# Sequence transforms of batches 1 to 3 of an FFT and MLP chain: three float32r products of two-part tables and folds in place of one float32 product

## The chip, the cores and the metric

The kernel runs on one core of a Trainium2 chip. The metric is device time in microseconds (us) of one execution. Times come from repeated executions; the profile is one further execution with the hardware profiler on. Engines are named as the profile names them: PE (TensorE, with PEld for its weight loads), DVE (VectorE), ACT (ScalarE), POOL (GpSimd), SP (SyncE, which here issues most DMAs).

## The reference

A two-dimensional Fourier transform of a real input, of which the real part is kept, then two feed-forward blocks:

```python
def _attn_ref(x):                       # x: (4, 3072, 256) float32
    X = np.fft.fft(x, axis=1)
    X = np.fft.fft(X, axis=2)
    return X.real.astype(np.float32)

def _moe_ref(x, w_in, w_out):           # (256, 2048), (2048, 256), drawn as float64
    h = x @ w_in
    g = np.maximum(0.01 * h, h)
    return (g @ w_out).astype(np.float32)

def _moe2_ref(x, mu_k, mu_r, w_k, w_v, w_r):
...
    k = np.maximum(xk @ w_k, 0.0)
    v = k * k @ w_v
    r = 1.0 / (1.0 + np.exp(-(xr @ w_r)))
    return (r * v).astype(np.float32)
```

## The kernel before, in words

**Four batches, four classes.** The transform along the 3072 positions of a batch uses the symmetry of real input. The positions are folded on each other (lines 162 to 221), so that a batch needs four products of a folded input with cosine or sine tables: kinds Pe, Qe, Po and Qo. Each kind is a sum over 768 rows, done as two halves of three 128-row pieces: `fft_a` (line 234) multiplies the first three pieces with the first table of the kind, `fft_b` (line 246) the other three with the second table. The result is 128 x 386. From the two halves ACT and DVE make two results each, which belong to classes A1, A2 (from Pe, Qe) and G1, G2 (from Po, Qo). The transform along the 256 channels is merged into `w_in` when the kernel starts.

**Steps.** A class is worked through in 16 steps, one for each 128 of the 2048 hidden columns, so a batch has 64 steps, numbered by `i` in the main loop. A step (`step`, line 537) puts on PE six products for the current hidden columns (three in `mm_b`, line 495, and three for the next step in `mm_a`, line 483) and twelve products with `w_out` (line 506) for the step two earlier. All of these are float32r: a float32 value is split by `hi_lo` (line 81) into two float32r parts, a leading part rounded by ACT and the rest by a DVE subtraction, and three products of parts stand for one product of float32. In a step DVE does `d` (line 547), `ev` (line 488, which `mm_b` of the next step waits for) and `gl` (line 527), ACT does `gh` and two leaky activations. After the 256 steps comes the second block, lines 816 to 872, which the change does not touch.

**What stands among the steps.** The sequence transforms are float32 products, three in each half, and the profile shows each of them as two PE instructions. Po is done at steps 2 and 3 of batch 0 and at steps 0 and 1 of the others, Qo at steps 10 and 11 or 3 and 4; Pe and Qe of the next batch at steps 53, 54 and 56, 57. `fft_a` is put behind the products of its step on PE, `fft_b` behind those of the step after. Pe has one extra float32 product with `e7p` (line 241), for the positions that fold on themselves.

**Tables.** There are eight tables of 128 x 3 x 386 float32 (579 KB each, `load_tab`, line 150), loaded by SP's queue into four rotating buffers, again for every batch. A buffer is loaded when PE has done its last product with it.

**Folds of the next batch.** For batch b+1 they go on during batch b, in six groups g. SP's queue loads half of the data into `eo` and `xl` (`first`, line 168), POOL's queue adds the other parts by four accumulating DMAs (`second`, line 180, each behind the one before it on the same tile), and DVE ends the group with three operations (`fin`, line 200): step 1 the difference of the `xl` halves into `eo` (line 202), steps 2 and 3 the sum into `plus` and the difference into `minus` (lines 204 and 206). The 18 `fin` steps are spread over the main loop's steps from f0 to f1: from 17 to 52 in batch 0, from 8 to 52 in the others. `first(0)`, `first(1)` and `second(0)` are issued behind `fft_b` of Qo.

**Other work among the steps.** At steps 53 to 57 and 0 to 4 a piece of the second block's weights is turned from float64 into two float32r parts (`w2_steps`, lines 96 to 145: DVE, ACT and two POOL operations). At step 1 of a class ACT copies the results of the class before out of PSUM.

The order on every engine is the order of the program text (the schedule is manual), and each engine takes its instructions in that order.

Of the kernel before, what the change touches and what calls it, by code (L numbers as in the profile page):

```python
# [17 lines left out]
P = 128  # L18
# [37 lines left out]
@with_exitstack  # L56
def fft_mlp_kernel(ctx, tc, xa, xb, x7, x8, x87, tb, alt, ce, so, mu, w_in, w_out, w_k, w_v, w_r, out):
    nc = tc.nc
# [103 lines left out]
    def fold_ops(b):  # L162
        plus = fft.tile([P, 6, 2, P], F32, tag="plus", bufs=1, name=f"plus{b}")
        minus = fft.tile([P, 6, 2, P], F32, tag="minus", bufs=1, name=f"minus{b}")
        folded[b] = {"Pe": plus[:, :, 0], "Qe": minus[:, :, 1], "Po": minus[:, :, 0], "Qo": plus[:, :, 1]}
        st, eo = {}, {}

        def first(g, p=None):
            if b == 0:
                t = st[g] = p.tile([P, 2, 2, D], F32, tag="xl", bufs=2 if p is fft else 4, name=f"xl{b}_{g}")  # L170
                Q.dma_start(t[:, 0], xa[b, g])
                Q.dma_start(t[:, 1], xb[b, g, :, :, 0:D])
            else:
                eo[g] = fft.tile([P, 2, 2, P], F32, tag="eo", bufs=2, name=f"eo{b}_{g}")
# [37 lines left out]
        def fold7(E=V):  # L212
            t = st["x7"]
            e7 = fft.tile([1, 2, P], F32, tag="e7", bufs=1, name=f"e7_{b}")
            o7 = fft.tile([1, 2, P], F32, tag="o7", bufs=1, name=f"o7_{b}")
            E.tensor_tensor(e7, t[:, :, :P], t[:, :, P:], op=ALU.add)
            E.tensor_tensor(o7, t[:, :, :P], t[:, :, P:], op=ALU.subtract)
            E.tensor_tensor(e7p[0:1], e7[:, 0], e7[:, 1], op=ALU.add)
            E.tensor_tensor(plus[0:1, 0, 1], o7[:, 0], o7[:, 1], op=ALU.subtract)

        return first, second, full, fin, load7, fold7

    folded, classes = {}, {}

# [7 lines left out]


    def fft_a(b, kind):
        t0 = KINDS[kind][0]
        src = folded[b][kind]
        ps = ps_s.tile([P, 512], F32, tag="s", name=f"f{b}{kind}")
        for c in range(3):
            T.matmul(ps[:, :JP], src[:, c], tabs[t0][:, c], start=(c == 0), stop=(c == 2 and kind != "Pe"))
        if kind == "Pe":  # L240
            T.matmul(ps[:, :JP], e7p, altt, start=False, stop=True)
        ev = work.tile([P, PJ], F32, tag="fv", bufs=2, name=f"fe{b}{kind}")
        act_copy(ev[:, :JP], ps[:, :JP])
        return ps, ev

    def fft_b(b, kind, ps, ev):
        _, t1, k1, k2 = KINDS[kind]
        src = folded[b][kind]
        for c in range(3):
            T.matmul(ps[:, :JP], src[:, 3 + c], tabs[t1][:, c], start=False, stop=(c == 2), skip_group_check=True)  # L250
# [129 lines left out]
    tabs = {}  # L380
    tcount = [0]

    def next_tabs(n=2):
        for _ in range(n):
            k = TORD[tcount[0] % 8]
            tcount[0] += 1
            tabs[k] = load_tab(k)

# [12 lines left out]
    for n, g in enumerate((0, 2, 1, 5, 3, 4)):  # L401
        first(g, fft if n < 2 else rows)
        if n == 2:
# [4 lines left out]
            Q.dma_start(altt[0:1], alt)  # L408
    next_tabs(2)
    w_out_load(0)  # L410
    next_tabs(2)
    w_in_load(2, True)
# [35 lines left out]
    wout[0][2]()  # L448
    next_tabs(2)
    w_in_parts(3)  # L450
    wout[1][1]()
    fft_b(0, "Qe", *qe)
    next_tabs(2)
    cur = split_class(0, A1, "P") + split_class(0, A1, "Q")
# [261 lines left out]
    for b in range(B):  # L716

        po_u, qo_u, f0, f1 = (2, 10, 17, 52) if b == 0 else (0, 3, 8, 52)
        pe_u, qe_u = 53, 56
        done = 0  # L720
        for ti, c in enumerate(CL):
# [3 lines left out]
            for u in range(NF):  # L725
# [10 lines left out]
                if b == 0 and ti == 0:  # L736
                    boot(u)
                if i == po_u:
                    half = fft_a(b, "Po")
                if i == po_u + 1:  # L740
                    fft_b(b, "Po", *half)
                    if b + 1 < B and b > 0:
                        next_tabs()
                if b == 0 and i == 6:
                    half = c_a(c8m, "c", False)
                if b == 0 and i == 7:
                    c_b(c8m, "d", G1, *half)
                    next_tabs()
                if i == qo_u:
                    half = fft_a(b, "Qo")  # L750
                if i == qo_u + 1:
                    fft_b(b, "Qo", *half)
                    if b + 1 < B:
# [4 lines left out]
                        second(0)  # L758
                        next_tabs()
                    else:  # L760
                        fft.release()
                        w2_alloc()
                if b + 1 < B:
                    while f0 <= i and done < 18 and done * (f1 - f0) < 18 * (i - f0 + 1):
                        g, q = divmod(done, 3)
                        fin(g, q + 1)
                        done += 1
                        if q == 0 and g < 5:
                            second(g + 1)
                        if q == 2 and g < 4:  # L770
                            first(g + 2)
                        if done == 12:
                            fold7(G)
                    if i == pe_u:
                        half = fft_a(b + 1, "Pe")
                    if i == pe_u + 1:
                        fft_b(b + 1, "Pe", *half)
                        next_tabs()
                    if i == qe_u:
                        half = fft_a(b + 1, "Qe")  # L780
                    if i == qe_u + 1:
                        fft_b(b + 1, "Qe", *half)
                        next_tabs()
                if b == 0 and i == 50:
# [155 lines left out]
def dft_tables():  # L940
# [31 lines left out]

    return f(tb), f(alt), f(lay(ce) / 256), f(lay(so) / 256)

# [33 lines left out]
```

## Time and profile before

| | us |
|---|---|
| median of 3 runs (lowest to highest) | 1549.6 (1549.31 to 1549.88) |
| the profiled execution, its own time | 1552.51 |
| span of the profiled execution, first to last instruction | 1550.6 |
| PE busy in the span | 1519.2 (98%) |
| DVE busy | 1064.5 (69%) |
| ACT busy | 917.0 (59%) |
| POOL busy | 161.8 (10%) |

The span is cut in 40 equal slices in the page. PE is busy in nine tenths or more of every slice but the first. The granted clock of PE is a tenth or more under full speed in the first slice alone, and its mean over the span is 0.992. The chain of work that ended last is made of PE for 94% of the span.

The profile's times of single matmuls include their run through the array, so neighbours overlap: what a product costs is read from the distance of starts, not from its duration.

### The profile page before, as it was taken

How to read it: one execution, taken by the hardware profiler on the slowest of the kernel's cores; microseconds unless marked ns; L12 is line 12 of the kernel's file. 1: busy time of each engine (PE TensorE's matmuls, PEld its weight loads, DVE VectorE, ACT ScalarE, POOL GpSimd, SP SyncE). 2: the span in 40 equal slices, each digit the busy share in tenths (PEclk: the TensorE clock that was granted, in tenths of full speed). 3: DMA queues.
4: the chain of work that ended last, by engine and by line, in shares of the span. 5: the costliest groups of instructions: out<-in, count | busy, mean ns of one | idle time of the engine just before them, and what ended most of it. 6: DMA issues, size and time to landing. Idle time of an engine off the chain costs nothing.

```text
span 1550.6 us, 22458 instructions
## 1 busy us (share of the span) xinstructions
PE 1519.2 (98%) x8418; PEld 1473.9 (95%) x8418; DVE 1064.5 (69%) x1783; ACT 917.0 (59%) x1761; POOL 161.8 (10%) x144
## 2 busy tenths in 40 slices
PE   5999999999999999999999999999999999999999
PEld 2789998999998999999999999999999999999998
DVE  7777775566775567766577675777777776777775
ACT  2666655556665555655566666666666666666664
POOL 4333110031200122200010000000000000000000
PEclk8999999999999999999999999999999999999999
DMA  7426412363402363212311001111111111111100
GB/s 245 154 72 135 81 31 77 108 136 57 80 26 90 99 118 57 56 42 74 107 53 26 22 21 42 41 50 49 48 50 42 42 42 41 42 42 42 41 21 31
DMA packets 75320, 102.12 MB, mean 66 GB/s; under 512 B 10798, under 2 KB 55870, under 8 KB 75210
## 3 DMA queue, kind: packets, MB, share of 16 engines
q1 hardware_dynamic: 55562, 88.85, 18.5%
q0 software_dynamic: 19648, 11.83, 5.9%
q8 instruction: 66, 1.08, 0.3%
q14 instruction: 44, 0.36, 0.1%
HBM read 72.83 MB, written 27.83 MB: 65 GB/s over the span
## 4 chain that ended last, share of the span: by engine, by line
PE 94%; DMA 2%; DVE 2%; issue 1%; ACT 1%; SPq 0%; POOL 0%; ACTq 0%; POOLq 0%; DVEq 0%
PE o L506 33%; PE kps L816 17%; PE v L857 17%; PE ps L495 8%; PE ps L483 8%; PE rps L865 4%; DMA xl<-in_xb 2%; PE wps L321 1%; DMA eo<-in_xa 0%; DMA xl<-in_xa 0%; PE cps L363 0%; PE cps L372 0%; DVE ev L488 0%; DVE d L547 0%; PE wps L323 0%
## 5 line engine op out<-in xcount | busy, mean ns | idle before, releaser
L547 DVE SCALAR_TENSOR_TENSOR d<-ev,ps 128x384 f32<-128x384 f32 (+1 forms) x256 | 142.0, 555 | 216.9 <-PE ps L495 216.4
L76 ACT ACTIVATE gh<-g 128x768 fp32r<-128x768 f32 (+1 forms) x256 | 216.3, 845 | 80.9 <-PE o L506 78.6
L820 ACT ACTIVATE rl<-kps 128x384 f32<-128x384 f32 x254 | 125.0, 492 | 218.5 <-PE kps L816 218.3
L79 ACT ACTIVATE g<-ps 128x384 f32<-128x384 f32 (+1 forms) x256 | 126.2, 493 | 211.6 <-DVE d L547 211.5
L527 DVE TENSOR_TENSOR gl<-g,gh 128x768 fp32r<-128x768 f32 (+1 forms) x256 | 249.5, 975 | 1.5 <-ACT gh L76 1.0
L821 DVE SCALAR_TENSOR_TENSOR k<-kps,rl 128x384 f32<-128x384 f32 x254 | 141.6, 558 | 137.7 <-ACT rl L820 133.8
L506 PE MATMUL o<-gh,uoh 128*128 128x384 f32 (+1 forms) x1024 | 230.4, 339 | 0.0
L506 PE MATMUL o<-gl,uoh 128*128 128x384 f32 (+1 forms) x1024 | 229.0, 338 | 0.0
L506 PE MATMUL o<-gh,uol 128*128 128x384 f32 (+1 forms) x1024 | 228.7, 337 | 0.0
L506 PEld LDWEIGHTS o<-gh,uoh 128*128 128x128 f32 x1024 | 184.3, 189 | 0.0
L506 PEld LDWEIGHTS o<-gh,uol 128*128 128x128 f32 x1024 | 183.8, 189 | 0.0
L506 PEld LDWEIGHTS o<-gl,uoh 128*128 128x128 f32 x1024 | 183.2, 188 | 0.0
L488 DVE SCALAR_TENSOR_TENSOR ev<-cb,w,ps 128x384 f32<-128x384 f32 (+1 forms) x256 | 157.2, 614 | 0.8 <-PE ps L483 0.8
L83 DVE TENSOR_TENSOR k2l<-k,k2h 128x384 fp32r<-128x384 f32 x254 | 139.6, 550 | 0.4 <-ACT k2h L76 0.4
L857 PE MATMUL v<-k2l,wvh 128*128 128x384 f32 x510 | 135.1, 336 | 0.0
L857 PE MATMUL v<-k2h,wvh 128*128 128x384 f32 x510 | 135.1, 336 | 0.0
L857 PE MATMUL v<-k2h,wvl 128*128 128x384 f32 x510 | 135.1, 336 | 0.0
L79 ACT ACTIVATE g<-d 128x384 f32<-128x384 f32 (+1 forms) x256 | 132.3, 517 | 0.0
L76 ACT ACTIVATE k2h<-k 128x384 fp32r<-128x384 f32 x254 | 131.3, 517 | 0.0
L816 PE MATMUL kps<-mh,wkh 128*128 128x384 f32 x508 | 129.6, 336 | 1.3 <-ACT mh L76 0.7
L816 PE MATMUL kps<-ml,wkh 128*128 128x384 f32 x508 | 129.5, 336 | 0.0
L816 PE MATMUL kps<-mh,wkl 128*128 128x384 f32 x508 | 129.4, 336 | 0.0
(295 smaller groups left out, 2501.3 us busy)
## 6 DMA issues: line engine op xcount, KB each, us to landing
out_dram<-o SPq DMA_DIRECT2D x31, 384.0 KB
y<-yo SPq DMA_DIRECT2D x24, 384.0 KB
xl<-in_xa SPq DMA_DIRECT2D x24, 256.0 KB
xa<-y SPq DMA_DIRECT2D x16, 384.0 KB
tab_a<-in_tb SPq DMA_DIRECT2D x8, 579.0 KB
tab_b<-in_tb SPq DMA_DIRECT2D x8, 579.0 KB
tab_c<-in_tb SPq DMA_DIRECT2D x8, 579.0 KB
tab_d<-in_tb SPq DMA_DIRECT2D x8, 579.0 KB
```

The costliest lines, as they stand in the source:

```text
L76: A.activation(o, i, ACTF.Copy)
L79: A.activation(o, i, ACTF.Prelu, alpha=0.01)
L83: V.tensor_tensor(lo, src, hi.bitcast(F32), op=ALU.subtract)
L483: T.matmul(x["ps"][:, :n], l[:, f], r[:, :n], start=(i == 0), stop=(i == 2))
L488: V.scalar_tensor_tensor(x["ev"][:, :n], x["cb"][:, :n], w128[:, u:u + 1], x["ps"][:, :n], op0=ALU.mult, op1=ALU.add)
L506: T.matmul(po[s][h][:, :n], w[:, u % HF, h * P:(h + 1) * P], g[:, s, :n], start=(u == 0 and i == 0), stop=(u == NF - 1 and i == 2))
L527: V.tensor_tensor(gl[:, :, :n], x["g"][:, :, :n], x["gh"][:, :, :n].bitcast(F32), op=ALU.subtract)
L547: V.scalar_tensor_tensor(d[:, :n], x["ev"][:, :n], 2.0, x["ps"][:, :n], op0=ALU.mult, op1=ALU.subtract)
L816: T.matmul(ps[:, :J], w[:, k, sl], x[:, k], start=(i == 0), stop=(i == 5))
L820: A.activation(r, ps[:, :J], ACTF.Relu)
L821: V.scalar_tensor_tensor(k2, ps[:, :J], 0.0, r, op0=ALU.max, op1=ALU.mult)
L857: T.matmul(vps[m][:, :J], w[:, f, m * P:(m + 1) * P], x, start=(f == 0 and i == 0), stop=(f == NK - 1 and i == 2))
```

## The change

For batches 1 to 3 each float32 product of a sequence transform becomes three float32r products: leading part of the fold by leading part of the table, leading part of the fold by rest of the table, rest of the fold by leading part of the table (`fft_mm`). Batch 0 keeps float32 products and float32 tables.

- Tables in two parts (`tbs`, 128 x 2 x 3 x 386, 1158 KB each) are computed on the host and loaded one by one by **POOL's** queue (`load_tab`), into **two** buffers. Batch 0's float32 tables come in pairs into the same two buffers (`load_pair_tab`), by SP's queue as before.
- The folds keep `eo` (the sums in place 0, the differences in place 1) for all six groups in one tile `pm`; `fin` steps 2 and 3 are gone for batches 1 to 3. Instead `fft_src` makes the 128 x 384 sum or difference `t` for one half of one kind (DVE), and splits it into `sh` (ACT) and `sl` (DVE). It is issued one step before `fft_a` for the first half and in the step of `fft_a` for the second.
- For batches 1 to 3 Po moves from steps 0, 1 to steps 1, 2 and Qo from 3, 4 to 4, 5. The six remaining `fin` operations (line 202 before, 214 after) of a batch go from step 17 to 50 in batch 0, and from **14** to 50 (from 8 to 52 before) in the others.

```diff
+    def load_pair_tab(k0, k1):
+        t = fft.tile([P, 2, 3, JP], F32R, tag="tab", bufs=2, name=f"tab_{k0}").bitcast(F32)
+        for i, k in enumerate((k0, k1)):
+            Q.dma_start(t[:, i], tb[TAB[k]])
+            tabs[k] = t[:, i]
+
     def load_tab(k):
-        t = fft.tile([P, 3, JP], F32, tag="tab", bufs=4, name=f"tab_{k}")
-        Q.dma_start(t, tb[TAB[k]])
-        return t
+        t = fft.tile([P, 2, 3, JP], F32R, tag="tab", bufs=2, name=f"tab_{k}")
+        G.dma_start(t, tbs[TAB[k]])
+        tabs[k] = t
...
     def fold_ops(b):
-        plus = fft.tile([P, 6, 2, P], F32, tag="plus", bufs=1, name=f"plus{b}")
-        minus = fft.tile([P, 6, 2, P], F32, tag="minus", bufs=1, name=f"minus{b}")
...
+        pm = fft.tile([P, 6, 2, 2, P], F32, tag="pm", bufs=1, name=f"pm{b}")
...
+            for g in range(6):
+                eo[g] = pm[:, g]
+            folded[b] = pm, o7s
...
+    def fft_src(b, kind, h):
+        pm, o7s = folded[b]
+        i = 0 if kind[0] == "P" else 1
+        t = work.tile([P, 3, P], F32, tag="fv", bufs=2, name=f"t{b}{kind}{h}")
+        hi = fft.tile([P, 3, P], F32R, tag="sh", bufs=2, name=f"sh{b}{kind}{h}")
+        lo = fft.tile([P, 3, P], F32R, tag="sl", bufs=2, name=f"sl{b}{kind}{h}")
+        s = pm[:, 3 * h:3 * h + 3, i]
+        V.tensor_tensor(t, s[:, :, 0], s[:, :, 1], op=ALU.add if kind in ("Pe", "Qo") else ALU.subtract)
...
+        hi_lo(hi, lo, t)
+        srcs[b, kind, h] = hi, lo
+
+    def fft_mm(b, kind, h, ps, stop):
...
+            hi, lo = srcs.pop((b, kind, h))
+            terms = [(w[:, c], t[:, i, c]) for c in range(3) for w, i in ((hi, 0), (hi, 1), (lo, 0))]
+        for n, (w, x) in enumerate(terms):
+            T.matmul(ps[:, :JP], w, x, start=(h == 0 and n == 0), stop=(stop and n == len(terms) - 1), **how)
...
-        po_u, qo_u, f0, f1 = (2, 10, 17, 52) if b == 0 else (0, 3, 8, 52)
+        po_u, qo_u, f0, f1 = (2, 10, 17, 50) if b == 0 else (1, 4, 14, 50)
...
+                for kb, kind, k_u in ((b, "Po", po_u), (b, "Qo", qo_u), (b + 1, "Pe", pe_u), (b + 1, "Qe", qe_u)):
+                    if kb == B:
+                        continue
+                    if kb > 0 and i in (k_u - 1, k_u):
+                        fft_src(kb, kind, i - k_u + 1)
+                    if i == k_u:
+                        half = fft_a(kb, kind)
+                    if i == k_u + 1:
+                        fft_b(kb, kind, *half)
+                    if kb > 0 and i in (k_u, k_u + 1):
+                        next_tab()
...
-                    while f0 <= i and done < 18 and done * (f1 - f0) < 18 * (i - f0 + 1):
-                        g, q = divmod(done, 3)
-                        fin(g, q + 1)
+                    while f0 <= i and done < 6 and done * (f1 - f0) < 6 * (i - f0 + 1):
+                        fin(done, 1)
+                        if done < 5:
+                            second(done + 1)
+                        if done < 4:
+                            first(done + 2)
                         done += 1
```

The order of the instructions shows it at three places. First PE, the first half of kind Pe of batch 1 (step 53 of batch 0) and what follows; `tab_a` is the table, `plus_1042` the fold. Before:

```order
L506 MATMUL o_2339<-gl,uoh 128x384
L239 MATMUL f1Pe<-tab_a,plus_1042 128x386 x3
L241 MATMUL f1Pe<-altt,e7p 128x386
L495 MATMUL ps<-Qh_3_2154,wh_122 128x384
L495 MATMUL ps<-Ql_3_2155,wh_122 128x384
```

With the change, where `sh1Pe_2389` and `sl1Pe_2390` are the two parts of the fold:

```order
L544 MATMUL o_2311<-gl,uoh 128x384
L272 MATMUL f1Pe<-tab_a,sh1Pe_2389 128x386 x2
L272 MATMUL f1Pe<-tab_a,sl1Pe_2390 128x386
L279 MATMUL f1Pe<-altt,e7p 128x386
L533 MATMUL ps<-Qh_3_2128,wh_122 128x384
```

The group of two rows on line 272 comes three times in the program, once for each 128-row piece; so nine float32r products take the place of three float32 ones, and the product with `e7p` stays float32.

Second DVE, steps 55 and 56 of batch 0, between `fft_b` of Pe and `fft_b` of Qe of batch 1. Before (`h` and `fv` belong to the second block's weights, `c1Pe` to the result of Pe):

```order
L256 SCALAR_TENSOR_TENSOR c1Pe_2491<-fe1Pe,c1Pe_2490 128x386
L109 SCALAR_TENSOR_TENSOR fv<-st,h 128x512
L547 SCALAR_TENSOR_TENSOR d<-ev,ps 128x384
L488 SCALAR_TENSOR_TENSOR ev<-cb_3_1859,w_124,ps 128x384
L527 TENSOR_TENSOR gl<-g,gh 128x2x384
L112 TENSOR_SCALAR h<-fv 128x512
```

With the change:

```order
L292 SCALAR_TENSOR_TENSOR c1Pe_2488<-fe1Pe,c1Pe_2487 128x386
L109 SCALAR_TENSOR_TENSOR fv<-st,h 128x512
L585 SCALAR_TENSOR_TENSOR d<-ev,ps 128x384
L526 SCALAR_TENSOR_TENSOR ev<-cb_3_1846,w_124,ps 128x384
L565 TENSOR_TENSOR gl<-g,gh 128x2x384
L256 TENSOR_TENSOR t1Qe_2525<-pm_1037 128x384
L83 TENSOR_TENSOR sl1Qe_2527<-t1Qe_2525,sh1Qe_2526 128x384
L112 TENSOR_SCALAR h<-fv 128x512
```

Two DVE operations come in behind `gl`; the second waits for ACT's `sh1Qe`, which waits for the first. The same pair stands behind `gl` of the next step, for the second half.

Third POOL's queue, from the last group of folds of batch 1 to the first of batch 2. Before:

```order
L185 DMA eo_5_1953<-in_xb 128x2x128
L116 TENSOR_TENSOR r<-st,h 128x512
L130 TENSOR_TENSOR r<-r,fv 128x512
L182 DMA eo_0_3021<-in_xa 128x2x128
L183 DMA xl_0_3022<-in_xb 128x2x256
```

With the change:

```order
L197 DMA pm_1037<-in_xb 128x2x128
L159 DMA tab_a_2443<-in_tbs 128x2316
L159 DMA tab_b_2491<-in_tbs 128x2316
L116 TENSOR_TENSOR r<-st,h 128x512
L159 DMA tab_c<-in_tbs 128x2316
L130 TENSOR_TENSOR r<-r,fv 128x512
L159 DMA tab_d<-in_tbs 128x2316
L159 DMA tab_c_2924<-in_tbs 128x2316
L159 DMA tab_d_2975<-in_tbs 128x2316
```

Behind these come a second `L116` and `L130`, two more tables and the accumulating DMAs of batch 2. `tab_a_2443` and `tab_b_2491` are the tables of Qe (the names drop the digit of `a2` and `b2`); each is issued when the buffer of `a` or `b`, which Pe used, comes free.

## Rows read from the trace of the kernel before

**Rows 1.** The page: engines' busy time, and the chain that ended last by engine
```profile
PE 1519.2 (98%) x8418; PEld 1473.9 (95%) x8418; DVE 1064.5 (69%) x1783; ACT 917.0 (59%) x1761; POOL 161.8 (10%) x144
...
PE 94%; DMA 2%; DVE 2%; issue 1%; ACT 1%; SPq 0%; POOL 0%; ACTq 0%; POOLq 0%; DVEq 0%
```

**Rows 2.** Timeline, PE around Qo of batch 1: start, duration, line, out<-in
```profile
300.21 0.34 PE L495 MATMUL ps<-Ql,wh 128*128 128x386 f32 x1
...
303.18 2.11 PE L239 MATMUL f1Qo<-tab_c,plus 128*128 128x386 f32 x6
...
305.30 0.34 PE L495 MATMUL ps<-Ql,wh 128*128 128x386 f32 x1
...
310.40 0.34 PE L495 MATMUL ps<-Ql,wh 128*128 128x386 f32 x1
...
313.56 0.34 PE L495 MATMUL ps<-Ql,wh 128*128 128x386 f32 x1
```

**Rows 3.** Waits: engine, line, what it waited for, us in total, times, longest
```profile
DVE eo L202 <- DMA xl<-in_xb: 9.0, 2, 4.5
```

**Rows 4.** Timeline, PE at the two long waits, in batches 1 and 2
```profile
323.02 0.34 PE L495 MATMUL ps<-Ql,wh 128*128 128x386 f32 x1
...
328.36 0.45 PE L495 MATMUL ps<-Qh,wh 128*128 128x386 f32 x1 [2.20 <-DVE ev L488]
...
333.36 0.34 PE L495 MATMUL ps<-Ql,wh 128*128 128x386 f32 x1
...
545.55 0.34 PE L495 MATMUL ps<-Ql,wh 128*128 128x386 f32 x1
...
555.96 0.34 PE L495 MATMUL ps<-Ql,wh 128*128 128x386 f32 x1
```

**Rows 5.** Stretches: us; busy of PE, PEld, DVE, ACT, POOL; PE clock; DMA share; GB/s
```profile
329.20:332.60 3.40, 3.40 (x12) 3.40 (x11) 2.82 (x5) 1.57 (x3) 2.27 (x3) 0.50 0.74 86
332.60:336.00 3.40, 3.40 (x21) 3.40 (x21) 2.02 (x3) 1.87 (x4) 1.10 (x1) 1.00 0.72 97
```

**Rows 6.** Timeline, POOL's issue of the late DMA, DVE's wait for it
```profile
316.43 1.11 POOL L183 DMA_DIRECT2D xl<-in_xb  x1
...
326.88 0.43 DVE L202 TENSOR_TENSOR eo<-xl 128x256 f32<-128x256 f32 x1 [4.45 <-DMA xl<-in_xb]
```

**Rows 7.** Groups of instructions, DVE and ACT: form, count, busy us, mean ns
```profile
L83 DVE TENSOR_TENSOR k2l<-k,k2h 128x384 fp32r<-128x384 f32 x254 | 139.6, 550 | 0.4 <-ACT k2h L76 0.4
...
L206 DVE TENSOR_TENSOR minus<-eo 128x256 f32<-128x256 f32 x22 | 10.2, 466 | 0.0
...
L76 ACT ACTIVATE k2h<-k 128x384 fp32r<-128x384 f32 x254 | 131.3, 517 | 0.0
```

**Rows 8.** Timeline, PE and DVE at steps 55 and 56 of batch 0
```profile
257.13 0.34 PE L495 MATMUL ps<-Qh,wh 128*128 128x384 f32 x1
...
256.77 0.95 DVE L527 TENSOR_TENSOR gl<-g,gh 128x768 fp32r<-128x768 f32 x1
257.64 0.42 DVE L112 TENSOR_SCALAR h<-fv 128x512 uint32<-128x512 uint32 x1
257.98 0.55 DVE L547 SCALAR_TENSOR_TENSOR d<-ev,ps 128x384 f32<-128x384 f32 x1
258.44 0.61 DVE L488 SCALAR_TENSOR_TENSOR ev<-cb,w,ps 128x384 f32<-128x384 f32 x1
```

**Rows 9.** Timeline, PE: end of Pe's first table, start of Qe's first half
```profile
248.24 0.81 PE L241 MATMUL f1Pe<-altt,e7p 128*128 128x386 f32 x2
...
260.28 2.11 PE L239 MATMUL f1Qe<-tab_a,minus 128*128 128x386 f32 x6
```

**Rows 10.** DMA queues (packets, MB, share of 16 engines), and accumulating DMAs of 128 KB
```profile
q1 hardware_dynamic: 55562, 88.85, 18.5%
q0 software_dynamic: 19648, 11.83, 5.9%
...
L182 POOL DMA_DIRECT2D eo<-in_xa x18: 1073/1082/1452, 118.6 to 635.1; - x18
...
DMA to landing us min/median/max: 3.2/3.5/8.9
```

More of the change, by code (lines that the diff above doesn't have):

```diff
@@ L56, in fft_mlp_kernel @@
 @with_exitstack
[L57 removed]
+def fft_mlp_kernel(ctx, tc, xa, xb, x7, x8, x87, tb, tbs, alt, ce, so, mu, w_in, w_out, w_k, w_v, w_r, out):
     nc = tc.nc
@@ L162, in fold_ops @@
     def fold_ops(b):
-        plus = fft.tile([P, 6, 2, P], F32, tag="plus", bufs=1, name=f"plus{b}")
-        minus = fft.tile([P, 6, 2, P], F32, tag="minus", bufs=1, name=f"minus{b}")
-        folded[b] = {"Pe": plus[:, :, 0], "Qe": minus[:, :, 1], "Po": minus[:, :, 0], "Qo": plus[:, :, 1]}
-        st, eo = {}, {}
+        st, eo, o7s = {}, {}, []
+        pm = fft.tile([P, 6, 2, 2, P], F32, tag="pm", bufs=1, name=f"pm{b}")
+        if b == 0:
+            plus, minus = pm[:, 0:3], pm[:, 3:6]
+            plus, minus = (t.rearrange("p g i o n -> p (g i) o n") for t in (plus, minus))
+            folded[b] = {"Pe": plus[:, :, 0], "Qe": minus[:, :, 1], "Po": minus[:, :, 0], "Qo": plus[:, :, 1]}
+        else:
+            for g in range(6):
+                eo[g] = pm[:, g]
+            folded[b] = pm, o7s
         def first(g, p=None):
@@ L218, in fold7 @@
             E.tensor_tensor(e7p[0:1], e7[:, 0], e7[:, 1], op=ALU.add)
-            E.tensor_tensor(plus[0:1, 0, 1], o7[:, 0], o7[:, 1], op=ALU.subtract)
+            if b == 0:
+                E.tensor_tensor(plus[0:1, 0, 1], o7[:, 0], o7[:, 1], op=ALU.subtract)
+            else:
+                o7s.append(o7)
         return first, second, full, fin, load7, fold7
-    folded, classes = {}, {}
+    folded, classes, srcs = {}, {}, {}
     KINDS = {
@@ L231, in fft_mlp_kernel @@
     }
+    def fft_src(b, kind, h):
[6 more added lines that the diff above has]
+        V.tensor_tensor(t, s[:, :, 0], s[:, :, 1], op=ALU.add if kind in ("Pe", "Qo") else ALU.subtract)
+        if kind == "Qo" and h == 0:
+            V.tensor_tensor(t[0:1, 0], o7s[0][:, 0], o7s[0][:, 1], op=ALU.subtract)
+        hi_lo(hi, lo, t)
+        srcs[b, kind, h] = hi, lo
+    def fft_mm(b, kind, h, ps, stop):
+        t = tabs[KINDS[kind][h]]
+        how = dict(skip_group_check=True) if h else {}
+        if b == 0:
+            src = folded[b][kind]
+            terms = [(src[:, 3 * h + c], t[:, c]) for c in range(3)]
+        else:
+            hi, lo = srcs.pop((b, kind, h))
+            terms = [(w[:, c], t[:, i, c]) for c in range(3) for w, i in ((hi, 0), (hi, 1), (lo, 0))]
+        for n, (w, x) in enumerate(terms):
+            T.matmul(ps[:, :JP], w, x, start=(h == 0 and n == 0), stop=(stop and n == len(terms) - 1), **how)
     def fft_a(b, kind):
-        t0 = KINDS[kind][0]
-        src = folded[b][kind]
         ps = ps_s.tile([P, 512], F32, tag="s", name=f"f{b}{kind}")
-        for c in range(3):
-            T.matmul(ps[:, :JP], src[:, c], tabs[t0][:, c], start=(c == 0), stop=(c == 2 and kind != "Pe"))
+        fft_mm(b, kind, 0, ps, kind != "Pe")
         if kind == "Pe":
@@ L246, in fft_b @@
     def fft_b(b, kind, ps, ev):
[L247 to L250, printed above, removed]
+        _, _, k1, k2 = KINDS[kind]
+        fft_mm(b, kind, 1, ps, True)
         nm = kind[0]
@@ L380, in fft_mlp_kernel, with next_pair, next_tab @@
     tabs = {}
[L381 to L387, printed above, removed]
+    pairs = [TORD[i:i + 2] for i in range(0, 8, 2)]
+    later_tabs = 3 * TORD
+    def next_pair():
+        load_pair_tab(*pairs.pop(0))
+    def next_tab():
+        if later_tabs:
+            load_tab(later_tabs.pop(0))
     x8t = fft.tile([P, 6, 4, 4], F32, name="x8t")
@@ L737, in fft_mlp_kernel @@
                     boot(u)
[L738 to L743, printed above, removed]
                 if b == 0 and i == 6:
@@ L747, in fft_mlp_kernel @@
                     c_b(c8m, "d", G1, *half)
-                    next_tabs()
-                if i == qo_u:
-                    half = fft_a(b, "Qo")
+                    next_tab()
[9 more added lines that the diff above has]
+                    if kb > 0 and i in (k_u, k_u + 1):
+                        next_tab()
                 if i == qo_u + 1:
-                    fft_b(b, "Qo", *half)
+                    if b == 0:
+                        next_tab()
                     if b + 1 < B:
@@ L763, in fft_mlp_kernel @@
                 if b + 1 < B:
-                    while f0 <= i and done < 18 and done * (f1 - f0) < 18 * (i - f0 + 1):
-                        g, q = divmod(done, 3)
-                        fin(g, q + 1)
-                        done += 1
[L768 to L772, printed above, removed]
-                            fold7(G)
[L774 to L783, printed above, removed]
+                    while f0 <= i and done < 6 and done * (f1 - f0) < 6 * (i - f0 + 1):
[4 more added lines that the diff above has]
+                            first(done + 2)
+                        done += 1
+                        if done == 4:
+                            fold7(G)
                 if b == 0 and i == 50:
```

21 lines of the change are left out of this document (12 added, 9 removed).

## The prediction, made before the changed kernel was run

> **What bounds the kernel now.** I read the page first. PE is busy for 98% of the span and makes up 94% of the chain that ended last; DVE is busy for 69% [rows 1]. So a microsecond counts when it leaves or enters PE's queue, or when another engine makes PE wait. I then went through PE's timeline for the pitch of its products and for places where a start comes late. The waits named one culprit that is not PE work, DVE's line 202 behind a DMA, twice [rows 3]; the timeline of those two places shows what it costs PE. The DMA queues come last, since the change puts large loads on POOL's.
>
> **Products: minus 8.6 us.** A plain step has 18 float32r products and takes 313.56 - 310.40 = 3.16 us from one `Ql` product to the next, 0.176 us for each. A step with half a sequence transform takes 305.30 - 300.21 = 5.09 and 310.40 - 305.30 = 5.10 [rows 2]. Three float32 products therefore cost 1.94 us. Nine float32r ones of the same 386 columns should cost 9 x 0.176 = 1.58 us, since the steps' products in these rows have that form and length, each with a weight load of its own. The gain is 0.36 us for one half; 3 batches x 4 kinds x 2 halves = 24 halves give 8.6 us. The `e7p` product stays float32 and costs what it did. Batch 0 gains nothing.
>
> **Folds: minus 8.1 us, through a wait that should go.** At step 8 of batches 1 and 2 the first `fin` is due. POOL issued the `xl` DMA at 316.43 and DVE got it at 326.88, having waited 4.45 us [rows 6]. `ev` stands behind `fin` in DVE's queue, and PE waits for `ev`: its product starts 2.20 us late by the row [rows 4]. Then the granted clock is half, 1.2 GHz, from 329.2 to 332.6 and full, 2.4 GHz, behind that [rows 5]; what PE did before it fell was to wait. From `Ql` to `Ql` two steps take 333.36 - 323.02 = 10.34 us, and 555.96 - 545.55 = 10.41 us at the second place [rows 4], where 6.32 would do: 4.0 and 4.1 us lost. With the change this `fin` is due at step 14. Its DMA is issued one step later, since Qo moves to steps 4 and 5, so five plain steps more, 15.8 us, lie between. The wait to be covered was 4.45 us; in front of it come two table loads more on the same queue, priced below at about 4 us each at the queues' common rate. 15.8 is more than 4.45 + 8, so I take the whole 8.1 us. At the other bound (nothing gained) the wait stays as it is.
>
> **DVE and ACT: nothing, but with a known cover.** Twelve `fin` operations a batch of 0.47 us go, 5.6 us; eight halves bring two DVE operations of 0.55 us, by the 128 x 384 row, and one ACT copy of 0.52 us, 8.8 and 4.1 us a batch [rows 7]. Busy time does not matter at 69%; order does. The tightest place is step 55, behind the late result of Pe: `gl` leaves DVE free at 257.64 [rows 8]. Now `t`, `sh`, `sl` run one behind the other: 0.55 + 0.52 + 0.55 = 1.62 us, with hand-overs about 1.8, so `sl` is done at about 259.4. The first half of Qe starts at 260.28 [rows 9] and needs it after two products. `h` (0.34 us to the next start) and `d`, `ev` follow: in the rows `ev` starts 0.80 us after `h` [rows 8] and lasts 0.61, so it ends at about 260.9. PE's next step starts at 257.13 + 3.16 + 1.58 = 261.87 (the PE row [rows 8], plus a step and a half transform). About 1 us is to spare, and that is the cover. If it is gone, `ev` is late next, and PE waits by the excess in each of the 24 halves. At the other steps the chain falls into a step that holds half a transform too, or has no weight work behind it; at step 1 ACT's four copies of the last class lie ahead of `sh`, and `sl` is only needed a step later.
>
> **Tables on POOL's queue: nothing, if one lands in time.** A load of 1158 KB is 1.19 MB, and no row shows such a load on this queue. The page's queue rows give bounds [rows 10]. Queue q1: 88.85 MB in 18.5% of 16 engines' 1550.6 us, so 310 GB/s with all engines at work, 3.8 us a table. Queue q0, which carries almost only accumulating DMAs: 11.83 MB in 5.9%, 129 GB/s, 9.2 us. To both come POOL's issue, 1.1 us, and a fixed part: 128 KB landed in 3.2 us at best, of which 1.0 is transfer at 129 GB/s, so 2.2 us. The buffer comes free at about 248.24, when Pe's first half is done, and Qe's first half starts at 260.28 [rows 9]: 12.0 us, 11.7 without the gain of the half between them. The second table of the pair is released 4.74 us later (a step and a half transform) and is needed 11.1 us after that. Sent one behind the other, a pair must have landed 15.8 us after the first release: 1.1 + 2.2 + 2 x 3.8 = 10.9 us at 310 GB/s, 4.9 us to spare. It holds up to 6.2 us a table, 190 GB/s. I take 310, because these loads write and do not add, and their rows of 9 KB are longer than those of the tables that q1 carried. POOL's other work there is two weight operations in five steps; the engine is busy 10% of the span [rows 1].
>
> The Trainium skill (DMA: Bandwidth & Descriptors, "Anatomy of one DMA - SWDGE (gpsimd) path") fits such a load as 2.0 us plus bytes over 436 GB/s, an estimate of 4.7 us for a table. The trace is slower where it can be compared: the fit gives 2.3 us for 128 KB, the row has 3.2 at best. The same page ("SWDGE vs HWDGE vs iDMA") says that a load into float32r always counts as a cast, which only this path does. It names no price for the cast, and no run here shows one. By the fit the sum stays as it is and the rival of late tables would lose its chance; the trace's slower landing is a reason that it keeps one.
>
> **SP's queue** loses the tables of batches 1 to 3. In batch 0 a pair of tables waits for two buffers instead of one, but the pair's second load stood behind its first in that queue before too, so what is queued behind them starts no later: nothing.
>
> **Sum.** 8.6 + 8.1 = 16.7 us. The profiled execution took 1552.5 us (span 1550.6), which becomes 1535.8; it stands 2.9 us above the median of the runs shown. Against the median of 1549.6 the forecast is **1532.9 us**.
>
> **Rivals.**
> - *The wait stays or moves* (the tables delay the folds' DMAs past step 14, or a later `fin` waits). For it: POOL's queue now has two table loads right ahead of `second(0)`, and that wait came in a stretch crowded by transfers. Against it: 15.8 us of new room. Products alone: 1541.0 us.
> - *DVE's chain runs late.* With 0.5 us of wait in each of 24 halves, 1544.9 us. For it: three engines hand over in series in a queue that has little slack behind `fft_b`. Against it: the 1 us worked out above.
> - *Tables land late, slower than before.* If a cast goes at the adding queue's 129 GB/s, a pair lands 1.1 + 2.2 + 18.4 = 21.7 us after the first release, 5.9 us late. There are six pairs whose buffers come free that late (Qe and Qo of three batches): 35 us, and each such wait would be followed by a stretch at half clock, 3.4 us long and 1.7 us lost by the rows of the old wait [rows 5], 10 us more: 1578 us. It decides from 6.2 us a table on; at 7.6 us (156 GB/s) the loss of 2.8 us a pair eats the whole gain. Against it: adding reads the target too, a load does not.
> - *The products do not go at one pass.* If the float32r products kept the float32 pitch (0.32 us an instruction, 1.94/6), a half would take 2.9 us and the time would be 1549.6 - 8.1 + 24 x 0.97 = 1565 us. The steps' own products, which take the same kinds of tile, speak against it.
>
> **Chances.** The forecast's case 0.76; the wait stays 0.07; DVE late 0.07; tables late 0.08, one in ten of it with a net loss too small to see; products slow 0.02. The forecast's own range is 1530 to 1536: 0.1 us more or less in each of 24 halves is 2.4 us. To hold 8 in 10 I reach to the rival of products alone, 1541.5, and leave the slow tables, the slow products and most of the late chain outside. A measurement tells about 0.2% from no change, 3 us. Faster by more than that: 0.76 + 0.07 + 0.07 = 0.90. Within: 0.01. Slower: 0.09.
>
> **What would show it.** Right: the half transforms show nine products in about 1.58 us; no wait of line 214 for `xl`, and no stretch at half clock between step 8 and the end of batches 1 and 2; PE does not wait for a table or for `sh`, `sl`. Wrong: PE rows on line 272 with idle time before them released by a DMA (tables) or by DVE or ACT (chain); half clock behind such a wait; `fin` waiting at step 14 or 20.

## The result, and the profile after

| | before | after |
|---|---|---|
| median of 4 runs (lowest to highest), us | 1549.74 (1549.31 to 1551.35) | **1535.41** (1534.1 to 1536.83) |
| the profiled execution, its own time | 1552.51 | 1535.28 |
| span | 1550.6 | 1533.5 |

The ratio is 0.990, 95% interval 0.9883 to 0.9917: faster by 14.3 us. The forecast was 1532.9 us with a range from 1530.0 to 1541.5. A second measurement of the changed kernel, on another chip (experiment r5), gave 1535.59 against 1551.2, ratio 0.9904 (0.989 to 0.9917). Two executions of the kernel before, on the chip of e1 to e4, ran at a mean clock of 0.56 and 0.76 and took 2520 and 2016 us; the ratios leave them out.

The page of after, engines' busy time and the chain that ended last by engine, against [rows 1]:

```profile
PE 1506.9 (98%) x8490; PEld 1480.5 (97%) x8490; DVE 1081.4 (71%) x1798; ACT 927.7 (60%) x1785; POOL 170.7 (11%) x165
...
PE 96%; DVE 2%; ACT 0%; issue 0%; DMA 0%; SPq 0%; POOL 0%; DVEq 0%; POOLq 0%; ACTq 0%
```

PE is still the bound. DVE, ACT and POOL are each busier, by 9 to 17 us, and the time fell all the same.

**The products.** Timeline of PE in after (start, duration, line, operation, tiles), steps 54 to 57 of batch 0, against [rows 2]:

```profile
252.03 0.34 PE L533 MATMUL ps<-Ql,wh 128*128 128x384 f32 x1
...
255.19 0.34 PE L533 MATMUL ps<-Ql,wh 128*128 128x384 f32 x1
...
258.17 0.51 PE L272 MATMUL f1Qe<-tab_a,sh1Qe 128*128 128x386 f32 x2
...
259.94 0.34 PE L533 MATMUL ps<-Ql,wh 128*128 128x384 f32 x1
...
264.67 0.34 PE L533 MATMUL ps<-Ql,wh 128*128 128x384 f32 x1
```

From `Ql` to `Ql` a plain step takes 255.19 - 252.03 = 3.16 us, as before. A step with half a transform takes 4.75 and 4.73 us, where it took 5.09 and 5.10. Nine products in 1.58 us is the predicted figure.

**The folds.** First PE's wait for `ev` in after (engine, line, what it waited for, us in total, times, longest); then `xl`'s DMA on POOL and the `fin` that uses it; then two stretches (columns as in [rows 5]):

```profile
PE ps L533 <- DVE ev L526: 2.3, 2, 1.5
```

```profile
319.59 1.48 POOL L195 DMA_DIRECT2D xl<-in_xb  x1
...
337.45 0.42 DVE L214 TENSOR_TENSOR pm<-xl 128x256 f32<-128x256 f32 x1
```

```profile
320.00:345.00 25.00, 25.00 (x145) 25.00 (x144) 17.19 (x28) 14.89 (x26) 10.94 (x10) 1.00 0.56 79
540.00:600.00 60.00, 60.00 (x344) 60.00 (x343) 40.74 (x64) 35.98 (x66) 18.58 (x17) 1.00 0.51 84
```

`fin` now starts 17.9 us after its DMA was issued (10.5 before, [rows 6]) and finds no wait in front of it: the bracket at the end of its row is gone. PE is busy through both stretches, at full clock. The 2.3 us that PE still waits for `ev` lie in the first 60 us.

**What the prediction did not have.** Step 4 of batch 1, just before the first half of Qo: POOL, DVE and PE.

```profile
298.23 1.31 POOL L116 TENSOR_TENSOR r<-st,h 128x512 f32<-128x512 f32 x1 [0.78 <-ACT st L115]
299.62 1.89 POOL L130 TENSOR_TENSOR r<-r,fv 128x512 f32<-128x512 f32 x1
```

```profile
299.00 1.36 DVE L565 TENSOR_TENSOR gl<-g,gh 128x772 fp32r<-128x772 f32 x1
300.29 1.64 DVE L256 TENSOR_TENSOR t1Qo<-pm 128x384 f32<-128x384 f32 x1
...
302.83 0.56 DVE L83 TENSOR_TENSOR sl1Qo<-t1Qo,sh1Qo 128x384 fp32r<-128x384 f32 x1 [0.59 <-ACT sh1Qo L76]
```

```profile
299.80 0.34 PE L533 MATMUL ps<-Ql,wh 128*128 128x386 f32 x1
...
302.85 0.62 PE L272 MATMUL f1Qo<-tab_c,sh1Qo 128*128 128x386 f32 x2
303.45 0.44 PE L272 MATMUL f1Qo<-tab_c,sl1Qo 128*128 128x386 f32 x1
...
304.97 0.34 PE L533 MATMUL ps<-Ql,wh 128*128 128x386 f32 x1
```

While POOL adds two operands for the weights, DVE's `t` takes 1.64 us; it takes 0.55 elsewhere. ACT gets `t` late, `sl` starts at 302.83 and PE, which wants it at about 303.2, is held up. The step takes 304.97 - 299.80 = 5.17 us, not 4.73. The waits name next to nothing here: the loss shows as slow first products (0.62 and 0.44 us), not as idle time. Batch 2 has the same (`t2Qo` 1.65 us), batch 3 has no weight work left: 0.9 us in all.

**Where the time came from, by these rows:** 8.6 us from products, some 8 us from the folds, 0.9 us given back at Qo. Between the two profiles the distances of the `Ql` rows, added up over all steps, agree: the steps with transforms of batches 1 to 3 became 7.6 us shorter, those between step 7 and step 52, with the folds, 8.1 us.

### The profile page after: what moved, and what is told of

Read it like the earlier page. It is cut to its first block, busy times and chain, and to the rows that moved or that the text cites. A ratio compares the mean times of both kernels' runs of the same rounds, so it can differ in the third digit from the quotient of the medians.

```text
span 1533.5 us, 22613 instructions
## 1 busy us (share of the span) xinstructions
PE 1506.9 (98%) x8490; PEld 1480.5 (97%) x8490; DVE 1081.4 (71%) x1798; ACT 927.7 (60%) x1785; POOL 170.7 (11%) x165
## 4 chain that ended last, share of the span: by engine, by line
PE 96%; DVE 2%; ACT 0%; issue 0%; DMA 0%; SPq 0%; POOL 0%; DVEq 0%; POOLq 0%; ACTq 0%
PE o L544 35%; PE kps L847 17%; PE v L888 17%; PE ps L533 9%; PE ps L521 9%; PE rps L896 4%; PE wps L357 1%; PE cps L399 0%; DMA xl<-in_xb 0%; DVE fe L205 0%; PE cps L408 0%; PE f0Qo L272 0%; DVE fo L206 0%; PE f0Po L272 0%; PE f2Qo L272 0%
```

## The experiments

All kernels were compared with the kernel before on their own chip. Rows of e2 and e3 have the line numbers of before, the others those of after; r7's are one higher from line 160 on. e1 to e4 ran on one chip, r5 to r8 on another, r9 on a third, where the kernel before took 1551.5, 1551.2 and 1550.2 us: a difference between runs of two chips is good to about a microsecond.

### e3: the kernel before, once more

No edit.

> The kernel before, unchanged, as a null run with a second profile. Theory of the gap between the profiles' difference (17.1 us) and the medians' difference (14.3 us): the first profile of before drew more half clock in the first 60 us than a usual execution does. Then this profile shows fewer or shorter stretches at half clock ahead of 60 us, and a span near 1548. Rival: the same stretches again and a span of 1550.6, so that the gap is in the changed kernel's spread. The comparison itself should give a ratio of 1.000 within 0.15%.

Measured: 1549.61 us (ratio 0.9996, 0.9984 to 1.0007). Single runs of the kernel before on this chip went from 1546.2 to 1554.0 us. The theory fits: the span is 1548.9 us, the first Pe product of batch 1 comes 2.2 us sooner than in the first profile (rows at "The sum" below), and the mean clock of the first 60 us is 0.89, against 0.86. The profile shows a second thing that varies. DVE's two waits, PE's `Ql` rows around them, and stretches behind them (columns as in [rows 5]):

```profile
324.63 0.43 DVE L202 TENSOR_TENSOR eo<-xl 128x256 f32<-128x256 f32 x1 [4.45 <-DMA xl<-in_xb]
...
546.51 0.42 DVE L202 TENSOR_TENSOR eo<-xl 128x256 f32<-128x256 f32 x1 [5.33 <-DMA xl<-in_xb]
```

```profile
320.78 0.34 PE L495 MATMUL ps<-Ql,wh 128*128 128x386 f32 x1
...
326.39 0.34 PE L495 MATMUL ps<-Ql,wh 128*128 128x386 f32 x1
...
541.77 0.34 PE L495 MATMUL ps<-Ql,wh 128*128 128x386 f32 x1
...
554.17 0.34 PE L495 MATMUL ps<-Ql,wh 128*128 128x386 f32 x1
```

```profile
328.40:331.80 3.40, 3.40 (x21) 3.40 (x20) 2.97 (x6) 2.24 (x5) 1.65 (x2) 1.00 0.91 118
...
548.40:551.80 3.40, 3.40 (x12) 3.40 (x12) 2.98 (x6) 1.99 (x4) 3.16 (x3) 0.50 0.39 49
551.80:555.20 3.40, 3.40 (x15) 3.40 (x14) 0.83 (x3) 0.85 (x1) 1.07 (x1) 0.67 0.79 106
```

The first wait is as long as in the first profile (4.45 us, [rows 6]), yet the clock stays full behind it, and PE loses 326.39 - 320.78 - 3.16 = 2.45 us between two `Ql` rows. Behind the second the clock is half for longer than in [rows 5], and PE loses 554.17 - 541.77 - 6.31 = 6.1 us. Together 8.5 us, against 8.1 in the first profile: the sum hardly differs, its parts do.

### e2: the kernel before, its first fold later

```diff
-        po_u, qo_u, f0, f1 = (2, 10, 17, 52) if b == 0 else (0, 3, 8, 52)
+        po_u, qo_u, f0, f1 = (2, 10, 17, 52) if b == 0 else (0, 3, 14, 52)
```

> The kernel before with its folds due from step 14 instead of 8 in batches 1 to 3, products still float32. Theory: the two waits for xl and both stretches at half clock behind them are gone, 8.1 us less than before by the profile, 1541.6 us. If the stretch at half clock does not follow the wait in every execution, the median gains less, down to 2 x 2.3 = 4.6 us, 1545 us. Rival (folds cost nothing on PE's path): 1549.7 us, as before.

Measured: 1542.15 us (ratio 0.9949, 0.9932 to 0.9966), 7.5 us under e3 and 9.4 under the median of all runs of the kernel before on that chip (1551.52). No wait of the fold for `xl` is left, no half clock behind the start phase, and a spread of 1.8 us (1541.8 to 1543.64). So the step at which the first fold is due is enough to bring the folds' 8.1 us, without the products and without the merged tile `pm`. What remains of the change, the products with all that comes with them, is the step from here to after: 6.6 us by the medians (1542.15 to 1535.59, on two chips) and 7.6 by the `Ql` rows.

### e1: the changed kernel, its first fold earlier

```diff
-        po_u, qo_u, f0, f1 = (2, 10, 17, 50) if b == 0 else (1, 4, 14, 50)
+        po_u, qo_u, f0, f1 = (2, 10, 17, 50) if b == 0 else (1, 4, 9, 50)
```

> The changed kernel with the first difference of a fold due at step 9 instead of 14 in batches 1 to 3, so four steps behind the second half of Qo, as before the change. Theory (the wait for the late load cost 8.1 us and its going is half of the gain): the wait of DVE for xl is back at step 9 of batches 1 and 2, 3 to 5 us each, PE loses 2 to 4.5 us at each place, so 1540 to 1544 us, products alone being worth 1541 by the prediction. Rival (the whole gain comes from the products, the stall was hidden or random): 1535 us as the changed kernel.

Measured: 1538.2 us (ratio 0.9925, 0.9909 to 0.994), 2.6 us over r5: the wait is back, at a lower price than the theory's 1540 to 1544 us, and the rival's 1535 is passed too.

```profile
324.92 0.43 DVE L214 TENSOR_TENSOR pm<-xl 128x256 f32<-128x256 f32 x1 [3.08 <-DMA xl<-in_xb]
541.99 0.43 DVE L214 TENSOR_TENSOR pm<-xl 128x256 f32<-128x256 f32 x1 [2.47 <-DMA xl<-in_xb]
```

DVE waits 3.08 and 2.47 us, and PE loses 1.55 and 0.95 us by its `Ql` rows (steps of 4.71 and 4.11 us, where 3.16 would do). That is 2.5 of the 3.0 us by which this profile's span exceeds that of after. The clock stays full behind both (1.00 from 326 to 334 and from 544 to 552 us). So the later step removes a wait, as predicted; the half clock is a second price beside it, which the old place paid at three of the four waits in the two profiles of the kernel before, and not here. The wait itself is shorter too. In before `xl` lands 10.4 us after POOL's issue [rows 6], with two tables and three pieces of weights sent off by SP within 1.3 us of it, and the DMA share until then is 1.05. In the changed kernel those loads go earlier, the DMA share is 0.59, and `xl` lands 5.1 us after its issue, at the second place 4.5. That the crowd of loads is the reason was not tested. Either way the old place costs 2.5 us in the changed kernel and 8 in before: without the later step the rest of the change would have taken a good part of the folds' gain.

Of the other 0.5 us, 0.36 went at the first half of Qo in batch 3, a step of 5.09 us where after has 4.73. Its table was issued at 726.99 and landed 10.8 us later, at 737.8; PE's first product with it starts at 737.88, with `sh` and `sl` long done. By these times it is a table that came late. The profile puts the 0.40 us for which PE's weight load sat idle there down to ACT's `g`, but in after the same weight load starts 0.35 us ahead of that `g`'s end, so it does not wait for it.

### r7: every table loaded twice

```diff
         G.dma_start(t, tbs[TAB[k]])
+        G.dma_start(t, tbs[TAB[k]])
```

> The changed kernel with every table of batches 1 to 3 loaded twice, the second load behind the first on POOL's queue. Theory (tables have about 4 us to spare, and late ones cost PE's time one for one): a table now lands 11 to 14 us after its release instead of 5.5 to 7.5, the first of a pair is up to 3 us late, the second 2 to 3 us later still; six pairs lose 3 to 6 us each, with or without 1.7 us of half clock: 1553 to 1580 us. Rival (the tables are far from any edge): within 2 us of the changed kernel.

Measured: 1583.02 us (ratio 1.0207, 1.0193 to 1.0221), 47.4 us over r5 and 3 us above the range expected. First two of POOL's issues in after, with the landing of its 24 loads of tables (us from issue, lowest, median, highest); then the second load in r7 and PE behind it:

```profile
246.95 0.58 POOL L159 DMA_DIRECT2D tab_a<-in_tbs  x1 [50.13 <-PE f1Pe L272]
...
724.39 0.53 POOL L159 DMA_DIRECT2D tab_c<-in_tbs  x1 [26.61 <-PE f3Po L272]
```

```profile
DMA to landing us min/median/max: 5.2/6.0/10.3
```

```profile
260.88 0.53 POOL L160 DMA_DIRECT2D tab_b<-in_tbs  x1 [7.40 <-DMA tab_b<-in_tbs]
```

```profile
266.43 0.59 PE L273 MATMUL f1Qe<-tab_b,sh1Qe 128*128 128x386 f32 x2 [3.44 <-DMA tab_b<-in_tbs]
```

```profile
276.20:279.60 3.40, 3.40 (x15) 3.40 (x14) 0.79 (x2) 0.92 (x2) 0.00 (x0) 0.67 1.01 382
```

With twice the bytes the rival of late tables comes true, and near its price (1578 us): PE's nine waits for tables, at all six pairs, sum to 31 us, and stretches at half clock follow, as in the last row (0.67 in the mean of that stretch). So tables can stop PE. In after no wait for one is in PE's list: `tab_a` of the rows above, issued at 246.95, lands 5.2 us later at 252.2 and is used at 258.17. How little is to spare elsewhere stands in the section on why the prediction was right.

### r8: two products for one instead of three

```diff
-            terms = [(w[:, c], t[:, i, c]) for c in range(3) for w, i in ((hi, 0), (hi, 1), (lo, 0))]
+            terms = [(w[:, c], t[:, i, c]) for c in range(3) for w, i in ((hi, 0), (lo, 0))]
```

> The changed kernel with two products in place of three in the transforms of batches 1 to 3: leading part by rest of the table is left out. Theory (a product costs its place in PE's queue, 0.176 us, and nothing hides it): 24 x 3 x 0.176 = 12.7 us less than the changed kernel, and the remaining six products of a half take 1.05 us. Rival (the products run beside something else, or weight loads or the DVE chain limit a half): less than half of that, because the fold's parts are then needed earlier and PE waits for them.

Measured: 1523.37 us (ratio 0.9827, 0.9813 to 0.984), 12.2 us under r5. PE at the same place:

```profile
254.14 0.34 PE L533 MATMUL ps<-Ql,wh 128*128 128x384 f32 x1
...
258.34 0.34 PE L533 MATMUL ps<-Ql,wh 128*128 128x384 f32 x1
```

A half of six products costs 4.20 - 3.16 = 1.04 us, 0.174 for each. Over the kernel 12.2 us for 24 x 3 = 72 products is 0.169 us each; a little of the gain goes at Qo, where less PE work covers the late `sl`. A product left out comes off the time whole, so PE is the bound, but for about 0.25 us at each of the first halves of Qo in batches 1 and 2.

### r9: sums, differences and parts made in the step that uses them

```diff
-                    if kb > 0 and i in (k_u - 1, k_u):
-                        fft_src(kb, kind, i - k_u + 1)
+                    if kb > 0 and i in (k_u, k_u + 1):
+                        fft_src(kb, kind, i - k_u)
```

> The sums, differences and parts of each half are made in the step of its products instead of one or two steps ahead, in all 21 or 24 halves that had a step's lead. Theory (the chain of VectorE, ScalarE and VectorE behind the copy out of PSUM takes some 1.7 to 1.8 us and is covered only by that lead): each half now stops TensorE for 0.8 to 1.2 us, 18 to 28 us in all, so 1553 to 1564 us, with waits of L272 for the parts at the head of the list. Rival (the chain lies beside other products wherever it is put): at most 1537 us.

Measured: 1565.81 us (ratio 1.0101, 1.0079 to 1.0122), 30 us over r5, or 1.26 us for each half.

```profile
261.28 0.55 DVE L256 TENSOR_TENSOR t1Qe<-pm 128x384 f32<-128x384 f32 x1
262.41 0.56 DVE L83 TENSOR_TENSOR sl1Qe<-t1Qe,sh1Qe 128x384 fp32r<-128x384 f32 x1 [0.59 <-ACT sh1Qe L76]
```

```profile
258.33 0.34 PE L533 MATMUL ps<-Ql,wh 128*128 128x384 f32 x1
...
262.44 0.62 PE L272 MATMUL f1Qe<-tab_a,sh1Qe 128*128 128x386 f32 x2 [0.97 <-ACT sh1Qe L76]
263.03 0.44 PE L272 MATMUL f1Qe<-tab_a,sl1Qe 128*128 128x386 f32 x1
...
264.55 0.34 PE L533 MATMUL ps<-Ql,wh 128*128 128x384 f32 x1
```

The chain is as long as predicted: `t` starts at 261.28, `sl` ends at 262.97, 1.7 us. Without the step's lead it stands on the path. My price for it was too low, since I counted the wait alone: the row says 0.97 us, but the step takes 264.55 - 258.33 = 6.22 us, 1.48 more than 4.74. The first products behind the wait take 0.59 and 0.28 us to the next start, where the same take 0.35 and 0.18 in an undisturbed half; and the idle time is counted from the end of the last product, though without a wait the next one would have started 0.17 us ahead of that end.

### e4 and r6: the weight work elsewhere

If POOL's weight work beside `t` costs 0.9 us at Qo, it should be movable. e4 puts it behind the transforms, r6 between the classes:

```diff
-                    if pe_u <= i < pe_u + 5 or (b > 0 and i < 5):
+                    if 58 <= i < 63 or (b > 0 and 6 <= i < 11):
```

> The changed kernel with the second block's weight pieces moved from steps 53 to 57 and 0 to 4 to steps 58 to 62 and 6 to 10, away from the fold sums and splits. Theory (POOL's two-operand work runs beside DVE's t of Qo and stretches it from 0.55 to 1.64 us, which makes PE wait 0.45 us at the first half of Qo in batches 1 and 2; the weights' last DVE operation makes PE wait 0.25 us behind Qe in batches 0 to 2): t is 0.55 us long everywhere, both waits go, 1.6 us less, 1533.8 us. Rival (t is long for the strided reads of pm, not for POOL): t of Qo stays at 1.6 us and the time at 1535.

Measured: 1538.28 us (ratio 0.9922, 0.9907 to 0.9938), 2.7 over r5: a miss. `t1Qo` and `t2Qo` are back at 0.55 us, so the rival of the strided reads is out, but a new wait came in batches 1 and 2. POOL's queue, then DVE:

```profile
323.27 1.07 POOL L197 DMA_DIRECT2D pm<-in_xb  x1 [2.54 <-DVE ev L526]
324.03 1.67 POOL L116 TENSOR_TENSOR r<-st,h 128x512 f32<-128x512 f32 x1
325.77 1.29 POOL L130 TENSOR_TENSOR r<-r,fv 128x512 f32<-128x512 f32 x1
```

```profile
327.10 0.69 DVE L134 SCALAR_TENSOR_TENSOR wl<-r,wh 128x512 fp32r<-128x512 f32 x1 [3.01 <-POOL r L130]
```

From step 6 on POOL's queue holds the adding DMAs of the fold, each of which waits for the one before it. The weights' two operations stand behind them, DVE's `wl` waits for those, and `ev` stands behind `wl`: the stall of the kernel before, with another cause. By the `Ql` rows the move saves 1.9 us at Qo and behind Qe (1.6 expected) and loses 3.8 in the two stalls.

r6 takes steps 46 to 50, where the last of these DMAs are out:

```diff
-                    if pe_u <= i < pe_u + 5 or (b > 0 and i < 5):
+                    if 58 <= i < 63 or (b > 0 and 46 <= i < 51):
```

> The changed kernel with the weight pieces moved to steps 58 to 62 and 46 to 50, where POOL's queue has neither folds nor tables in front of them. Theory (the run with steps 6 to 10 was slow because the weights' last DVE operation waited for POOL, whose queue stood behind the adding DMAs of the folds): no DVE wait for POOL, no wait at Qo's first half, none of the 0.25 us behind Qe, so 1.6 us less than the changed kernel on the same chip, 0.999 of it. Rival (moving the weights at all costs as much as it saves): the same time as the changed kernel or more.

Measured: **1533.43 us** (1531.92 to 1533.59; ratio 0.9888, 0.9875 to 0.9902), 2.2 us under after on the same chip (r5: 1535.59, 1534.11 to 1536.8). No run of the one reaches a run of the other. At Qo:

```profile
299.22 0.55 DVE L256 TENSOR_TENSOR t1Qo<-pm 128x384 f32<-128x384 f32 x1
```

```profile
302.46 0.52 PE L272 MATMUL f1Qo<-tab_c,sh1Qo 128*128 128x386 f32 x2
302.82 0.33 PE L272 MATMUL f1Qo<-tab_c,sl1Qo 128*128 128x386 f32 x1
```

`t` takes 0.55 us again and PE's first product runs at the usual pitch. Of the 2.2 us, 0.9 are the two Qo. The step behind Qe went from 3.51 us, which before has too, to 3.16 in each of three batches, 1.0 us. This is the fastest version that ran with all three products.

### r5: the changed kernel, once more

No edit; the measure for r6 to r9.

> The changed kernel, unchanged, as the measure for the other three of this call and a second profile of it. Theory: ratio to before 0.990, no stretch at half clock between 100 us and the end, 0.45 us of wait at the first half of Qo in batches 1 and 2 again. Rival (its gain over before depends on the chip or on luck with the clock): a ratio outside 0.988 to 0.992.

Measured: 1535.59 us, ratio 0.9904, as expected. The clock is 1.00 from 60 us to the end, and Qo's 0.45 us stand at the same two places.

## Why the prediction was right

**Products, minus 8.6 us: right.** 1.94 us became 1.58 (timeline of after), in 24 places, and r8 shows that this time is PE's, but for some 0.5 us at Qo. The rival of slow products is out.

**Folds, minus 8.1 us: right in sum and cause, the working too neat.** e2 takes this gain alone, by one number, and measures 7.5 to 9.4 us. I took "4.0 and 4.1 us" as the price of two equal stalls, each with 3.4 us at half clock. In e3 the two cost 2.45 and 6.1 us: no half clock behind the first, half clock for longer than 3.4 us behind the second. In e1, where the wait is 3.08 and 2.47 us, there is none. That the price came out right is in part luck, since it is a sum of two draws. The cover was also more than was needed: `xl` lands 4.8 us after its issue (10.4 before) and `fin` starts 17.9 us after it, so some 13 us are to spare. The prediction had the tables ahead of it as a delay only.

**DVE and ACT, nothing: right at the place worked out, wrong at one that was waved through.** At step 55 of after the chain runs as predicted:

```profile
254.65 0.95 DVE L565 TENSOR_TENSOR gl<-g,gh 128x768 fp32r<-128x768 f32 x1
255.52 0.55 DVE L256 TENSOR_TENSOR t1Qe<-pm 128x384 f32<-128x384 f32 x1
256.66 0.56 DVE L83 TENSOR_TENSOR sl1Qe<-t1Qe,sh1Qe 128x384 fp32r<-128x384 f32 x1 [0.59 <-ACT sh1Qe L76]
```

From `t` to the end of `sl` it takes 1.70 us (1.8 predicted), and PE uses `sl` after 258.17. r9 shows that the lead of one step is what hides it, and what it would cost without: 30 us. The sentence that failed is "At the other steps the chain falls into a step that holds half a transform too, or has no weight work behind it". At step 4 the weight work is not behind the chain in DVE's queue but beside it, on POOL, and I looked at queues only. The missing term is 0.9 us.

The Trainium skill (SBUF — State Buffer, "Who interferes with whom") says that a VectorE instruction with two inputs in SBUF contends with a GpSimd instruction that reads SBUF, that the ports they share are an exclusive lock, and that the order of issue decides who is blocked. The rows agree, three times in turn. POOL's multiplication runs from 298.23 to 299.54; `gl`, started at 299.00, ends at 300.36, 0.82 us after it, and takes 1.36 us where it takes 0.95 elsewhere. POOL's addition, started at 299.62 behind `gl`, ends at 301.51, after 1.89 us, where e4 has 1.29. `t`, started at 300.29, ends at 301.93, 0.42 us after the addition, and lasts 0.55 when it runs alone (r6). Spans on POOL are rough, so the ends can't be read closer than that. By this rule, weighed before, the term would have been in the sum: these operations have two inputs in SBUF.

**Tables, nothing: right, with a margin of 0.3 us at most that I had not worked out.** I put 1.1 us for the issue and 2.2 + 3.8 = 6.0 us to landing; the rows have 0.53 to 0.67 and 5.2 to 10.3 us. PE never waits for a table in after. The pair that I worked out has 6.0 us to spare at its first table. (I had its second table released 4.74 us behind the first. The `e7p` product lies between, the second is issued 5.37 us behind the first, and the pair's room was 0.6 us more than the 15.8 of the prediction.) The pair from Po to Qo, which I did not work out, has next to nothing. Its first table lands 9.2 us after its issue in batch 1, with 1.5 us to spare. In batch 3 it was issued at 724.39, landed 10.3 us later at 734.7, and was used at 735.01:

```profile
735.01 0.52 PE L272 MATMUL f3Qo<-tab_c,sh3Qo 128*128 128x386 f32 x2
```

The DMA engines are busy 96% of that stretch, against 66% while the first table of Qe in batch 1 lands in 5.2 us. So that the term is nothing is in part luck: in e1 the same load took 0.5 us more and PE lost 0.36 us. r7 shows the rival's mechanism, and its price was fair: 47 us measured where 35 + 10 were worked out.

The Trainium skill's fit for this path (DMA: Bandwidth & Descriptors, "Anatomy of one DMA - SWDGE (gpsimd) path") gives 4.7 us for such a load, an estimate from its figures. The trace does not agree: the fastest load here took 5.2 us, the slowest 10.3, so the fit is low by 0.5 to 5.6 us.

**The sum.** 16.7 us predicted, 0.9 given back: 15.8. The medians differ by 14.3 us in the first measurement and by 15.6 in r5's; 15.8 lies within the interval of both. So of the 2.5 us by which the forecast's time was low, 0.9 are Qo, and for the other 1.6 no run shows a place; it is within what the measurement can tell. The forecast was worked out from a profiled execution 2.9 us above its median, and I took that excess off at the end. The profile of after had no such excess (1535.28, the median 1535.41), so the two spans differ by 17.1 us: 7.6 from the steps with transforms, 8.1 from those with folds, and 1.4 from ahead of the first Pe product of batch 1. That product's start, in the kernel before, in e3 and in after:

```profile
246.29 2.11 PE L239 MATMUL f1Pe<-tab_a,plus 128*128 128x386 f32 x6
```

```profile
244.06 2.11 PE L239 MATMUL f1Pe<-tab_a,plus 128*128 128x386 f32 x6
```

```profile
244.88 0.52 PE L272 MATMUL f1Pe<-tab_a,sh1Pe 128*128 128x386 f32 x2
```

Up to there the first two are the same program, 2.2 us apart: the profile of before drew a long start phase. Taking its excess off was right in kind. That after starts 0.8 us later than e3 and r5 1.2 us earlier than after says that a microsecond or so of the difference between any two executions is of this sort.

## What to carry to other kernels

Count what an added operation meets on the other engines, not only in its own queue: two engines that read the same memory side by side can stretch a 0.55 us operation to 1.64. A chain over three engines costs nothing if it is issued one step ahead, and 1.26 us a time if it is not. Before work is moved to a quieter place, look at what its own engine's queue holds there: behind POOL's adding DMAs (e4) the weight work lost 2.7 us, and elsewhere (r6) it saved 2.2. Read a load's landing at the place where it is needed, not in a median over places: 6.0 us in the median was 10.3 where it counted, with 0.3 to spare.

## What was unexpected

- POOL beside DVE: an addition on POOL made `t` three times as long (1.64 instead of 0.55 us), and the multiplication ahead of it made `gl` 1.36 instead of 0.95 us. The second is no effect of the change: the kernel before has `gl` at 1.36 beside the same operation, without a loss.
- The half clock behind a wait is no fixed price. After the same 4.45 us wait of DVE it came for 3.4 us in one execution of the kernel before and not at all in another; behind a 3.08 us wait of PE (e3) it lasted longer than 3.4 us, behind the losses of 1.55 and 0.95 us in e1 it did not come.
- A wait costs PE more than its idle time: the row of r9 has 0.97 us, the step loses 1.48.
